# Three weight-sharing projection chunks, scores by key block and a later flag read in a fused attention kernel

## The chip, the cores and the metric

The kernel runs on one core of a Trainium2 chip. The metric is the device time of one execution in microseconds (us). A timed execution is 1.8 us longer than the span that its profile shows from the first to the last instruction.

The engines: PE (TensorE) multiplies, PEld is its weight load, ACT is ScalarE, DVE is VectorE, POOL is GpSimd, SP is SyncE, which here issues all 611 DMAs. Each engine has a program of its own.

## The reference

```python
B, Sq, D = 8, 112, 640
H, Sk, Dh = 32, 512, 192
q = (x @ wq).reshape(B, Sq, H, Dh).transpose(0, 2, 1, 3)
scores = einsum("bhqd,bhkd->bhqk", q, k_cache) * Dh ** -0.5
o = einsum("bhqk,bhkd->bhqd", softmax(scores), v_cache)
out = o.transpose(0, 2, 1, 3).reshape(B, Sq, H * Dh) @ wo
```

All is bf16. The key and value caches are 50 MB each, so about 118 MB have to be read.

## The kernel before

The work is cut into 64 units (8 groups of 4 heads, times 8 batches). For each unit DVE transposes four key blocks, PE makes scores, ACT takes the exponential, PE multiplies by the values, and output and projection matmuls of other groups fill in. POOL copies three quarters of each unit's values into a padded tile and reorders projection weights. The program starts with the projection of group 0, in six chunks `c` of two halves `h`. It ends with a check flag: each engine reads it and branches to the end, or to a slower second program if a row sum was out of range.

```python
def get_flag(eng):                        # every engine's last act
    W(eng, vT, 3)                         # W = wait for a semaphore
    eng.reg_load(regs[eng.engine], flag[0:1, 0:1])
...
def do_Q0_first():                        # PE: chunks 0 and 1, first half
    for dc in range(DC):                  # five pieces of weights
        W(pe, mW0[dc], 16)                # landed?
        for c in range(2):
            for a in range(4):            # one "group" of four matmuls
                ... pe.matmul(ps[32*a:32*a+32, 6 + c, 0:HQ], ...)
def do_Q0(c, h):                          # the other chunks
    W(pe, aQ, n - 1)                      # ACT has emptied the bank of chunk n-2
    ... into bank 6 + n % 2               # chunks 4, 5 use weights that POOL reorders
...
def do_S(u):                              # PE: scores of unit u
    W(pe, vKT, 4 * (u + 1))               # for unit 0: all four key blocks
    W(pe, aEX, 4 * u)                     # all exponentials of unit u-1
...
def exp(u, a):                            # ACT
    W(act, pS, 4 * u + a + 1)
    if a == 3 and u >= 2:
        W(act, gM, u + 1)                 # POOL has copied unit u's values
...
def middle(u):                            # POOL: that copy
    W(gp, mV[u % NV], 64 * (u // NV + 1)) # the values have landed
...
# POOL's loop: reorder projection weights placed at u, then a check, then middle(u + 2)
EARLY_LOADS = ("k1", "q", "v0", "k2", "v1", "k3", "o", "v2")   # SP's order of issue after k0
```

Of the kernel before, what the change touches and what calls it, by code (L numbers as in the profile page):

```python
# [666 lines left out]
def build_main(nc, x, k_cache, v_cache, wq, wo, out, flag, regs, hints):  # L667
# [8 lines left out]
    HQ = R // 2  # L676
# [19 lines left out]
    o_list = [(g, m, h) for g in range(NG) for m in range(MT) for h in range(2)]  # L696
# [61 lines left out]
    with ExitStack() as es:  # L758
# [7 lines left out]
        xT = sb("xT", [128, DC, R], BF16)  # L766
        wqs = sb("wqs", [128, 2, DC, 4 * DH], BF16)
# [6 lines left out]
        qT = [sb(f"qT{j}", [128, 6, R], BF16) for j in range(2)]  # L774
# [3 lines left out]
        wq0 = oT[:].rearrange("p c r -> p (c r)")[:, 0:DC * 4 * DH].rearrange("p (d w) -> p d w", d=DC)  # L778
# [11 lines left out]
        ps = es.enter_context(nc.psum_tensor("ps", [128, 8, 512], F32))  # L790
# [11 lines left out]
        aX, aEX, aQ, aT, aNM = (sem(n) for n in ("aX", "aEX", "aQ", "aT", "aNM"))  # L802
# [14 lines left out]
        def W(eng, s, v):  # L817
            if v > 0:
                eng.wait_ge(s, v)

        def bank_free(eng, pair, h):
# [3 lines left out]
            else:  # L825
                W(eng, vO, o_index[g, c, h] + 1)

        def last_unit(m):
            return -(-128 * (m + 1) // SQ) - 1

        def get_flag(eng):
            W(eng, vT, 3)
            eng.reg_load(regs[eng.engine], flag[0:1, 0:1])

        def on_tensor(pe):
            def do_X(m):
                if m in (0, 2, 4):
                    W(pe, mX[x_piece[m]], 16)
                if m == 6:
                    W(pe, aQ, 5)  # L840
                for dc in range(DC):
                    mm = pe.transpose(psb[:, 5 if m == 3 and dc >= 2 else m, dc * 128:(dc + 1) * 128], xs[:, m, dc * 128:(dc + 1) * 128], ident[:])  # L842
                mm.then_inc(pXT, 1)
# [8 lines left out]
            def do_Q0_first():  # L852
                W(pe, vX, 3)
                W(pe, aX, 2)
                for dc in range(DC):
                    W(pe, mW0[dc], 16)
                    for c in range(2):
                        for a in range(4):
                            w0 = DH * a + 64 * (c // 2) + c % 2
                            mm = pe.matmul(ps[32 * a:32 * a + 32, 6 + c, 0:HQ], wqs[:, 0, dc, w0:w0 + 63:2],  # L860
                                           xT[:, dc, 0:HQ], start=(dc == 0), stop=(dc == DC - 1))
                        if dc == DC - 1:
                            mm.then_inc(pQ, 1)

            def do_Q0(c, h):
                n = q_index[0, c, h]
                if c == 0:
                    W(pe, vX, 4)
                    W(pe, aX, 4)
                W(pe, aQ, n - 1)  # L870
                for dc in range(DC):
                    if h == 1 or c >= RAW:
                        if h == 0 and c == RAW:
                            W(pe, gW0, dc + 1)
                        mm = pe.matmul(ps[:, 6 + n % 2, 0:HQ], wq0[:, dc, 128 * c:128 * (c + 1)], xT[:, dc, HQ * h:HQ * (h + 1)],  # L875
                                       start=(dc == 0), stop=(dc == DC - 1))
                        continue
                    for a in range(4):
                        w0 = DH * a + 64 * (c // 2) + c % 2
                        mm = pe.matmul(ps[32 * a:32 * a + 32, 6 + n % 2, 0:HQ], wqs[:, 0, dc, w0:w0 + 63:2],  # L880
                                       xT[:, dc, HQ * h:HQ * (h + 1)], start=(dc == 0), stop=(dc == DC - 1))
                mm.then_inc(pQ, 1)

# [37 lines left out]
            def do_S(u):  # L921
                g, b = divmod(u, B)
                if u < 3 or kt_ahead[u - 2][0] + min(3, kt_ahead[u - 2][1] - kt_ahead[u - 2][0]) < 4 * (u + 1):
                    W(pe, vKT, 4 * (u + 1))
                if b == 0 or u == 4:
                    W(pe, aQ, q_index[g, 5, b // 4 if g == 0 else 1] + 1)
                W(pe, aEX, 4 * u)
                if u == 0:
                    W(pe, vX, 3)
                    W(pe, aX, 2)  # L930
                for t in range(4):
                    for c in range(6):
                        for a in range(4):
                            p = slice(32 * a, 32 * a + 32)
                            mm = pe.matmul(ps[:, a, SQ * t:SQ * (t + 1)], kt[u % NT][p, t, c // 2, :, c % 2],  # L935
                                           qT[g % 2][p, c, SQ * b:SQ * (b + 1)], start=(c == 0), stop=(c == 5))
                            if t == 3 and c == 5:
                                mm.then_inc(pS, 1)
# [36 lines left out]
            for j in range(BRIDGE):  # L975
                (held if j else pe.matmul)(ps[:, 7, 0:128], wt[:], wt[:], True, True)
            do_Q0_first()
            for c in range(2, 6):
                do_Q0(c, 0)
            for m in range(4, MT):  # L980
                do_X(m)
# [21 lines left out]
        def on_scalar(act):  # L1003
            W(act, vI, 1)
            act.activation(dmy[:, 1:2], dmy[:, 0:1], ACTF.Exp)

            def evac_x(m, n=DC):
                W(act, pXT, m + 1)
                act.activation(xT[:, 0:n, 128 * m:128 * (m + 1)],
                               psb[:, m, 0:128 * n].rearrange("p (c s) -> p c s", c=n), ACTF.Copy).then_inc(aX, 1)  # L1010

            def evac(g, c, h):
                n = q_index[g, c, h]
                W(act, pQ, n + 1)
                if g >= 2 and c == 0 and h == 0:
                    W(act, pS, 4 * B * (g - 1))
                act.activation(qT[g % 2][:, c, HQ * h:HQ * (h + 1)], ps[:, 6 + (n % 2 if g == 0 else h), 0:HQ],  # L1017
                               ACTF.Copy).then_inc(aQ, 1)

            def evac_pair(i, j):  # L1020
                if slot[i, j] and slot[i, j][0][0] == "Q" and slot[i, j][1] != FRONT:
                    for h in range(2):
                        evac(*slot[i, j][0][1:], h)

            def exp(u, a):
                W(act, pS, 4 * u + a + 1)
                if a == 3 and u >= 2:
                    W(act, gM, u + 1)
                if a == 0:
                    W(act, pPV, u - 1)  # L1030
                    if u < 2:
                        W(act, gV, 1)
                act.activation(pT[u % 2][:, a, :, 0:SQ], ps[:, a, 0:4 * SQ].rearrange("p (t q) -> p t q", t=4), ACTF.Exp,  # L1033
                               scale=scale).then_inc(aEX, 1)

            def norm(u):
                W(act, vRC, u + 1)
                W(act, pT_, u - 1)
                for e in range(2):
                    ins = act.activation(os_[u % 2][:, DH * (2 + e):DH * (3 + e)], pv_of(u)[0:SQ, 1, e, 0:DH], ACTF.Copy,  # L1040
                                         scale=rinv[:, u % 4, 2 + e:3 + e])
                ins.then_inc(aNM, 1)

            def tevac(u):
                g, b = divmod(u, B)
                W(act, pT_, u + 1)
                if g > 0:
                    W(act, pO, 2 * (MT * (g - 1) + (SQ * b + SQ - 1) // 128 + 1))
                src = psb[:, bank_of_T(u), 2:2 + 4 * RW].rearrange("p (k w) -> p k w", k=2)[:, :, 0:3 * SQ]
                act.activation(oT[:, :, SQ * b:SQ * (b + 1)].rearrange("p (k c) q -> p k c q", k=2),  # L1050
                               src.rearrange("p k (c q) -> p k c q", c=3), ACTF.Copy).then_inc(aT, 1)

            evac_x(1)
            evac_x(3, 2)
            for c in range(6):
                evac(0, c, 0)
            for m in (4, 5):
                evac_x(m)
            for c in range(6):
                if c < 4:  # L1060
                    exp(0, c)
                evac(0, c, 1)
            for i in range(1, NU + 2):
                if i == HINT_AT["act"]:
                    hints[mybir.EngineType.Activation] = act.mark_branch_hint_location()
                if i < NU:
                    exp(i, 0)
                if i >= 2:
                    tevac(i - 2)
                if i < NU:  # L1070
                    exp(i, 1)
                evac_pair(i, 0)
                if i < NU:
                    exp(i, 2)
                    exp(i, 3)
                if 1 <= i <= NU:
                    norm(i - 1)
                evac_pair(i, 1)
            get_flag(act)
# [276 lines left out]
```

## Time and profile before

| | before |
|---|---|
| timed runs at first, median (range) | 396.77 us (396.52 to 397.45) |
| span of the profile | 396.5 us |
| PE busy | 387.3 us |
| first projection matmul to first score matmul | 7.68 us |
| end of the last output addition to the end of the span | 3.05 us |
| issue of the last output DMA | 1.39 us (that of the one before: 0.33) |

From the page of the profile of the kernel before: the span, the busy times, and the chain that ended last as shares of the span.

```profile
span 396.5 us, 19831 instructions
...
PE 387.3 (98%) x8865; PEld 242.6 (61%) x8262; DVE 283.2 (71%) x506; ACT 250.6 (63%) x550; POOL 153.3 (39%) x352
...
PE 97%; issue 1%; DMA 1%; DVE 1%; ACT 0%
```

PE is busy almost always, and the chain of what released what hardly leaves it.

The chain of waits of the kernel before, 3 to 17 us, in order of time: start, duration, what. L860 is `do_Q0_first`, L880 and L875 the other chunks, L842 the transposes of x, L935 the scores, L1017 the eviction of a chunk by ACT.

```profile
6.54 2.22 PE ps L860 x36
8.75 0.02 issue
8.78 0.55 ACT qT L1017
9.33 0.04 issue
9.37 2.08 PE ps L880 x40
11.45 2.00 PE ps L875 x10
13.45 0.84 PE ps L842 x15
14.29 1.04 PE ps L935 x75
15.33 0.76 issue
```

Two holes: PE stands from 8.75 to 9.37 us while ACT empties the first bank, and for 0.76 us inside the first scores, where the chain names no releaser ("issue").

The end, from the timeline of the kernel before: SP's last DMA issue (start, duration).

```profile
393.50 1.39 SPq L1299 DMA_DIRECT2D out_dram<-xs  x1
```

And the DMA view of the kernel before from 393.45 us on: packets of the instruction queue q8, and the one issue in this stretch with its time to landing.

```profile
q8 instruction: 1, 0.02, 1.8%
...
out_dram<-xs SPq DMA_DIRECT2D x1, 64.0 KB, 2.9
```

One packet of 16384 bytes falls on the same time as the last issue (it starts at 393.50 and takes 1.05 us), and the output needs 2.9 us to land. I take q8 for PE's instruction queue: it has 69 packets in the run, all of 16384 bytes, and six gaps of PE inside its scores follow such a packet: PE goes on 2.25 to 3.2 us after its start (median 2.5). All six lie at the same place when PE's 17180 records are counted off in 256s (at 193 to 195), and 17180 divided by 256 makes 67. I call these gaps packet gaps (the recorded texts say fetch gaps, or instruction fetch). That PE stands there for want of the packet is read from the coincidence in time and place.

### The profile page before, as it was taken

What the parts mean: (1) busy time and instruction counts of PE and PEld (TensorE: products, weight loads), DVE (VectorE), ACT (ScalarE), POOL (GpSimd) and SP (SyncE); (2) the same over time, 40 slices, a digit from 0 to 9 for tenths busy, and PEclk for the clock granted to TensorE, in tenths of its full rate; (3) what the DMA queues carried; (4) which work ended last, traced back from release to release, by engine and by line L of the source; (5) the groups of instructions that cost most, each with busy time, mean ns of one, the idle gap of its engine ahead of it and who ended that gap; (6) DMA issues with size and microseconds to landing.
All of it is one profiled execution on the core that took longest, in us unless ns stands there. A gap on an engine that the chain in (4) does not pass through costs nothing.

```text
span 396.5 us, 19831 instructions
## 1 busy us (share of the span) xinstructions
PE 387.3 (98%) x8865; PEld 242.6 (61%) x8262; DVE 283.2 (71%) x506; ACT 250.6 (63%) x550; POOL 153.3 (39%) x352
## 2 busy tenths in 40 slices
PE   7999999999999999999999999999999999999995
PEld 2555665656656656666666656666566665667672
DVE  1664778677796777776787676876678677789733
ACT  3667665757647765657755666566764766667562
POOL 5433454233442354334342255233454223334420
PEclk9999999999999999999999999999999999999999
DMA  8999999999999999899999999999999889989712
GB/s 263 376 370 374 355 302 366 331 311 351 323 367 292 311 309 358 282 312 304 306 293 345 307 275 337 365 275 317 282 292 345 257 271 317 339 274 297 254 35 72
DMA packets 88588, 120.04 MB, mean 303 GB/s; under 512 B 9776, under 2 KB 88496, under 8 KB 88496
## 3 DMA queue, kind: packets, MB, share of 16 engines
q1 hardware_dynamic: 88496, 118.72, 91.0%
q8 instruction: 69, 1.13, 1.2%
q14 instruction: 23, 0.19, 0.2%
HBM read 117.54 MB, written 1.15 MB: 299 GB/s over the span
## 4 chain that ended last, share of the span: by engine, by line
PE 97%; issue 1%; DMA 1%; DVE 1%; ACT 0%
PE ps L953 22%; PE ps L916 22%; PE ps L846 22%; PE ps L935 21%; PE ps L964 6%; PE ps L875 2%; DMA xs<-in_x_dram 1%; PE ps L842 1%; PE ps L860 1%; PE ps L880 1%; DVE xs L1115 0%; DVE xT L1120 0%; ACT qT L1017 0%
## 5 line engine op out<-in xcount | busy, mean ns | idle before, releaser
L1092 DVE STREAM_TRANSPOSE kt<-kr 128x384 int32<-128x384 int32 x256 | 195.4, 871 | 9.7 <-DMA kr<-in_k_cache_dram 9.7
L1033 ACT ACTIVATE pT<-ps 128x448 bf16<-128x448 f32 x256 | 130.4, 559 | 85.2 <-PE ps L935 85.1
L935 PEld LDWEIGHTS ps<-qT,kt 32*128 32x128 bf16 x6144 | 77.3, 93 | 33.3 <-issue 23.1
L916 PE MATMUL ps<-wos,oT 128*128 128x320 bf16 (+2 forms) x342 | 93.0, 298 | 0.7 <-DVE xs L1115 0.7
L1212 POOL TENSOR_SCALAR bad<-rinv 112x4 f32<-112x4 f32 x64 | 14.7, 230 | 201.7 <-DVE rinv L1098 201.7
L953 PE MATMUL ps<-vm,pT 128*128 128x193 bf16 x768 | 91.5, 247 | 0.2
L935 PE MATMUL ps<-qT,kt 32*128 32x112 bf16 x6144 | 88.6, 208 | 2.8 <-issue 2.8
L846 PE MATMUL ps<-wos,oT 128*128 128x320 bf16 (+1 forms) x340 | 91.3, 296 | 0.0
L953 PEld LDWEIGHTS ps<-vm,pT 128*128 128x128 bf16 x768 | 67.8, 97 | 21.2 <-ACT oT L1050 11.1
L1195 POOL COPY vm<-vs 128x1152 int32<-128x1152 int32 x64 | 73.5, 1149 | 13.3 <-issue 6.2
L846 PE MATMUL ps<-xT,wqs 128*128 128x448 bf16 (+2 forms) x226 | 74.1, 341 | 0.0
L916 PE MATMUL ps<-xT,wqs 128*128 128x448 bf16 (+1 forms) x210 | 73.5, 350 | 0.0
L1040 ACT ACTIVATE os<-ps,rinv 112x192 bf16<-112x192 f32 x128 | 48.0, 437 | 28.5 <-DVE rinv L1098 28.5
L953 PE MATMUL ps<-vs,pT 128*128 128x193 bf16 x256 | 62.6, 245 | 0.0
L916 PEld LDWEIGHTS ps<-wos,oT 128*128 128x128 bf16 x342 | 33.2, 97 | 43.8 <-issue 36.7
L1017 ACT ACTIVATE qT<-ps 128x448 bf16<-128x448 f32 x96 | 47.9, 552 | 18.9 <-PE ps L916 12.3
L1115 DVE TENSOR_TENSOR acc<-ps,acc 128x320 f32<-128x320 f32 x84 | 37.3, 486 | 26.3 <-PE ps L916 26.0
L1050 ACT ACTIVATE oT<-ps 128x672 bf16<-128x672 bf16 x64 | 46.4, 725 | 2.1 <-PE ps L964 2.1
L1098 DVE RECIPROCAL rinv<-ps 112x4 f32<-112x4 f32 x64 | 11.1, 174 | 50.1 <-PE ps L953 50.1
L916 PEld LDWEIGHTS ps<-xT,wqs 128*128 128x128 bf16 x210 | 20.3, 97 | 34.2 <-issue 29.4
L1101 DVE TENSOR_TENSOR os<-ps,rinv 112x384 bf16<-112x384 f32 x64 | 35.7, 558 | 7.3 <-DVE rinv L1098 0.5
L1188 POOL COPY wqs<-wqr 128x384 bf16<-128x384 bf16 x70 | 33.4, 511 | 5.4 <-DMA wqr<-in_wq_dram 5.4
(44 smaller groups left out, 155.1 us busy)
## 6 DMA issues: line engine op xcount, KB each, us to landing
kr<-in_k_cache_dram SPq DMA_DIRECT2D x256, 192.0 KB, 4.2
vs<-in_v_cache_dram SPq DMA_DIRECT2D x256, 192.0 KB, 4.1
wos<-in_wo_dram SPq DMA_DIRECT2D x48, 160.0 KB, 4.3
wqr<-in_wq_dram SPq DMA_DIRECT2D x35, 192.0 KB, 5.3
wqs<-in_wq_dram SPq DMA_DIRECT2D x5, 192.0 KB, 4.6
out_dram<-xs SPq DMA_DIRECT2D x6, 160.0 KB, 2.5
xs<-in_x_dram SPq DMA_DIRECT2D x2, 320.0 KB, 3.5
xs<-in_x_dram SPq DMA_DIRECT2D x1, 480.0 KB, 5.7
```

What stands on the lines that cost most here:

```text
L846: return pe.add_instruction(mybir.InstMatmult(name=nc.get_next_instruction_name(), engine=mybir.EngineType.PE, ins=[pe.lower_ap_or_imm(rhs ...
L916: mm = (pe.matmul if h == hs[0] and f == 0 else held)(ps[:, 6 + h, cs], w, rhs[h][:, cs], q == 0, q == n - 1 and f == cuts - 1)
L935: mm = pe.matmul(ps[:, a, SQ * t:SQ * (t + 1)], kt[u % NT][p, t, c // 2, :, c % 2], qT[g % 2][p, c, SQ * b:SQ * (b + 1)], start=(c == 0), ...
L953: mm = pe.matmul(pv[:, k, e, 0:DH + 1], pT[u % 2][:, a, t, :], src[:, a, v0:v0 + DH + 1], start=(t == 0), stop=(t == 3), skip_group_check= ...
L1017: act.activation(qT[g % 2][:, c, HQ * h:HQ * (h + 1)], ps[:, 6 + (n % 2 if g == 0 else h), 0:HQ], ACTF.Copy).then_inc(aQ, 1)
L1033: act.activation(pT[u % 2][:, a, :, 0:SQ], ps[:, a, 0:4 * SQ].rearrange("p (t q) -> p t q", t=4), ACTF.Exp, scale=scale).then_inc(aEX, 1)
L1040: ins = act.activation(os_[u % 2][:, DH * (2 + e):DH * (3 + e)], pv_of(u)[0:SQ, 1, e, 0:DH], ACTF.Copy, scale=rinv[:, u % 4, 2 + e:3 + e])
L1050: act.activation(oT[:, :, SQ * b:SQ * (b + 1)].rearrange("p (k c) q -> p k c q", k=2), src.rearrange("p k (c q) -> p k c q", c=3), ACTF.Co ...
L1092: dve.transpose(dst, src).then_inc(vKT, 1)
L1101: dve.tensor_tensor(os_[u % 2][:, 0:2 * DH].rearrange("p (e d) -> p e d", e=2), pv[0:SQ, 0, :, 0:DH], rinv[:, u % 4, 0:2][:, :, None].broa ...
L1115: ins = dve.tensor_tensor(ob[:, m, cs] if g == NG - 1 else acc[:, m, cs], src, acc[:, m, cs], op=ALU.add)
L1195: gp.tensor_copy(vm[u % NM][:].rearrange("p a (t w) -> p a t w", w=RW)[:, :, :, 0:DH].bitcast(I32), vs[u % NV][:, :, 32:32 + 3 * DH].rearr ...
```

## The change

The intent: let three chunks use each piece of weights as it lands, in three banks, so that PE needn't wait for an eviction; let the first scores wait for one key block at a time; and keep every engine from reading the flag until the last output addition.

```diff
+        def bank_of_Q0(n):
+            return (6, 7, 0, 5, 4, 7)[n] if n < 6 else 6 + n % 2
         def get_flag(eng):
+            W(eng, vO, len(o_list))
             W(eng, vT, 3)
@@ do_X
-                if m == 6:
+                if m in (4, 5, 6):
                     W(pe, aQ, 5)
@@ do_Q0_first
-                    for c in range(2):
+                    for c in range(3):
...  (6 + c, 6 + n % 2 become bank_of_Q0, in ACT's eviction too)
@@ do_Q0
-                W(pe, aQ, n - 1)
+                W(pe, aQ, (0, 0, 0, 0, 0, 2)[n] if n < 6 else n - 1)
@@ do_S
-                    W(pe, vKT, 4 * (u + 1))
+                    W(pe, vKT, 4 * (u + 1) if u else 1)
...
                 for t in range(4):
+                    if u == 0:
+                        W(pe, vKT, t + 1)
@@ PE's order
-            for c in range(2, 6):
+            for c in range(3, 6):
                 do_Q0(c, 0)
```

More of the change, by code (lines that the diff above doesn't have):

```diff
@@ L856, in do_Q0_first @@
                     W(pe, mW0[dc], 16)
-                    for c in range(2):
+                    for c in range(3):
                         for a in range(4):
                             w0 = DH * a + 64 * (c // 2) + c % 2
-                            mm = pe.matmul(ps[32 * a:32 * a + 32, 6 + c, 0:HQ], wqs[:, 0, dc, w0:w0 + 63:2],
+                            mm = pe.matmul(ps[32 * a:32 * a + 32, bank_of_Q0(c), 0:HQ], wqs[:, 0, dc, w0:w0 + 63:2],
                                            xT[:, dc, 0:HQ], start=(dc == 0), stop=(dc == DC - 1))
@@ L874, in do_Q0 @@
                             W(pe, gW0, dc + 1)
-                        mm = pe.matmul(ps[:, 6 + n % 2, 0:HQ], wq0[:, dc, 128 * c:128 * (c + 1)], xT[:, dc, HQ * h:HQ * (h + 1)],
+                        mm = pe.matmul(ps[:, bank_of_Q0(n), 0:HQ], wq0[:, dc, 128 * c:128 * (c + 1)], xT[:, dc, HQ * h:HQ * (h + 1)],
                                        start=(dc == 0), stop=(dc == DC - 1))
@@ L879, in do_Q0 @@
                         w0 = DH * a + 64 * (c // 2) + c % 2
-                        mm = pe.matmul(ps[32 * a:32 * a + 32, 6 + n % 2, 0:HQ], wqs[:, 0, dc, w0:w0 + 63:2],
+                        mm = pe.matmul(ps[32 * a:32 * a + 32, bank_of_Q0(n), 0:HQ], wqs[:, 0, dc, w0:w0 + 63:2],
                                        xT[:, dc, HQ * h:HQ * (h + 1)], start=(dc == 0), stop=(dc == DC - 1))
@@ L1016, in evac @@
                     W(act, pS, 4 * B * (g - 1))
-                act.activation(qT[g % 2][:, c, HQ * h:HQ * (h + 1)], ps[:, 6 + (n % 2 if g == 0 else h), 0:HQ],
+                act.activation(qT[g % 2][:, c, HQ * h:HQ * (h + 1)], ps[:, bank_of_Q0(n) if g == 0 else 6 + h, 0:HQ],
                                ACTF.Copy).then_inc(aQ, 1)
```

## The prediction

> **What bounds the kernel now.** The tensor engine (PE). The page gives PE busy 387.3 of 396.5 us, clock granted 1.0, and the chain of waits is 97% PE. The instruction records show only twelve PE gaps over 0.04 us. Six of them (2.8 us) are inside the score matmuls and follow the 16 KB packets of the instruction queue by about 2.45 us; the rest lie in the first 10 us and the last 8. After 17 us PE never stands still for a load, so a shift of PE's start should reach the end.
>
> **Start (timeline and chain, 4 to 17 us).** The weights of the first projection land at 5.80, 6.33, 7.31, 7.81, 8.31 us, and two chunks (2 groups of four matmuls, 0.208 us a group by the third and fourth chunks: 2.08 us for 10) consume each: 6.54 to 8.75. PE's weight load waits 0.31 to 0.38 us for the last three. Then the chain leaves PE: chunk 2 waits for the first ACT eviction (8.78 to 9.33) and starts at 9.37. Projection ends 13.45, transposes 14.29, then scores.
> With three chunks in three banks the first pass is 15 groups, 3.12 us: each weight costs 0.62 us, more than the 0.50 between arrivals, so waits vanish: 6.54 to 9.66. Chunks 3 and 4 have own banks and no eviction wait; chunk 5's bank 7 is free by about 10.3. PE runs through to about 12.70, transposes to 13.54. New limits do not bind by my sum: POOL's reordered weights end 10.50 (chunk 4 starts 10.70); x's last piece lands 11.75 (needed 12.70); chunk 4's eviction ends about 12.3; chunk 5's at 13.3. Scores start about 13.55 instead of 14.29: gain 0.75 us. The key transposes end at 11.2, 11.95, 12.7, 13.44, so waiting per key block gains about nothing[...]. The 0.76 us gap in the first scores[...] should stay. Next consumers have slack: keys of unit 2 are ready 1.8 us before use.
>
> **End (trace's DMA and SyncE records, 390 to 396.5 us).** ACT, POOL and PE read the flag at 391.55 and branch at 392.1 while output is still coming. PE's branch is followed by a 16 KB instruction packet at 393.50 (1.05 us). The last output's DMA issue starts at 393.50 and takes 1.387 us instead of 0.33; it lands at 396.37 and ends the span. Throughout the run long DMA issues (1 to 2 us against 0.43) coincide with these packets. One piece of the output before has a straggler (395.57 against 394.61). [...] The change moves the branches behind the last addition (393.47): flag read to about 394.05, PE's packet about 395.4, after the last issue (now done at 393.83) and about at its landing (393.83+1.45=395.3). Gain about 1.05 us of span. [...]
>
> **Sum.** 396.77-0.7-0.95: about 395.1 us; 8 in 10: 394.4 to 396.2. Faster by over 2%: 0.005; within: 0.99; slower: 0.005.
>
> **What would show it.** No PE gap near 9.4 and scores starting near 13.5; weight-load waits on the first weights gone; the last output issue near 0.33 us, no instruction packet between 392 and 395; the last addition about 0.7 us earlier and the span 1.7 shorter.
>
> **What would make it wrong.** Instruction packets falling elsewhere and stalling scores or issues by another 1 us; the flag-waiters' packets hitting the last landing; a new wait of the transposes for evictions; loads limiting units 1 to 3, giving the 0.7 back.

The sum came to 396.77 - 0.7 - 0.95 = 395.1 us. In it 0.75 us of the start count as 0.7, and 1.05 us of the end as 0.95.

## The result, and the profile after

| | before | after |
|---|---|---|
| median of 6 runs (range) | 396.63 us (395.40 to 397.45) | 394.86 us (394.36 to 395.59) |
| span of the profile | 396.5 us | 392.6 us |
| first projection to first scores | 7.68 us | 6.74 us |
| last addition to end | 3.05 us | 1.71 us |
| gaps of PE inside score matmuls, sum | 2.83 us | 1.92 us |

The ratio is 0.9964, 95% interval 0.9943 to 0.9986. A ratio is the mean time of one kernel's runs over the mean of the other's from the same rounds, so it is not quite the ratio of the medians in the table. The two profiles differ by 3.9 us, more than twice the timed difference: the profile of before fell on an execution slower than all six timed ones (398.36 us), that of after on the fastest of its six (394.36). So the two spans must not simply be subtracted.

From the page of the profile after, the same lines.

```profile
span 392.6 us, 19835 instructions
...
PE 385.5 (98%) x8865; PEld 242.2 (62%) x8262; DVE 283.2 (72%) x506; ACT 250.7 (64%) x550; POOL 153.0 (39%) x352
...
PE 91%; SPq 3%; issue 2%; DMA 2%; DVE 1%; POOL 0%; ACT 0%; ACTq 0%
```

PE's share of the chain fell from 97% to 91%, and SP's queue and a DMA came in. This is the line to stop at: the chain's beginning is no longer PE's.

PE's timeline of the kernel after, 6.6 to 13.6 us (L864 is `do_Q0_first`, L884 and L879 the other chunks, L846 the transposes, L941 the scores).

```profile
6.74 3.02 PE L864 MATMUL ps<-xT,wqs 128*32 128x448 bf16 x60
9.59 1.12 PE L884 MATMUL ps<-xT,wqs 128*32 128x448 bf16 x20
10.64 2.06 PE L879 MATMUL ps<-xT,oT 128*128 128x448 bf16 x10
12.54 1.00 PE L846 MATMUL ps<-ident,xs 128*128 128x128 bf16 x15
13.47 0.33 PE L941 MATMUL ps<-qT,kt 32*128 32x112 bf16 x12
```

No hole is left in this stretch. Sixty matmuls take 3.02 us, and the next chunks follow at once.

The timeline of the kernel after, SP's last issue.

```profile
390.87 0.33 SPq L1305 DMA_DIRECT2D out_dram<-xs  x1
```

The DMA view of the kernel after from 390.85 us on.

```profile
out_dram<-xs SPq DMA_DIRECT2D x1, 64.0 KB, 1.5
```

The issue takes 0.33 us instead of 1.39, and the output lands 1.5 us after the issue began instead of 2.9. PE's instruction packet comes only at 392.76, when the output has landed (392.40).

So both ends changed as they were meant to. But the chain of waits of the kernel after, 17 to 34 us, reads like this (many issues of SP left out; L1301 is SP's issue of loads, L1201 POOL's copy, L1039 the exponential):

```profile
23.92 0.43 SPq L1301
24.35 0.04 issue
24.39 1.10 DMA vs<-in_v_cache_dram
25.49 4.87 issue
30.36 1.15 POOL vm L1201
31.52 0.02 issue
31.54 0.02 ACTq L819
31.56 0.04 issue
31.60 0.55 ACT pT L1039
32.16 0.14 issue
32.29 1.21 PE ps L941 x82
```

Read it upwards. The scores of unit 3 (32.29) waited for the last exponential of unit 2, that one for POOL's copy of unit 2's values, the copy for those values to land (30.25), and the load had been issued from 22.97 us on because SP had been issuing one DMA after another since 0.7 us. SP's order of issue is not the whole of it: the last of these four DMAs was issued at 24.39 us and landed 5.9 us later (the first x, issued at 0.74, took 3.8), and from 20 to 30 us the 16 DMA engines were fully taken (busy share 1.07, 371 GB/s), so the transfers probably stood in line too. No work of PE is in this chain before 32.29 us, so it doesn't depend on when PE started. The question for the experiments was how much of the start's gain goes through it.

### The profile page after: what moved, and what is told of

It reads as the page before. It is cut to its first block, busy times and chain, and to the rows that moved or that the text cites. A ratio compares the mean times of both kernels' runs of the same rounds, so it can differ in the third digit from the quotient of the medians.

```text
span 392.6 us, 19835 instructions
## 1 busy us (share of the span) xinstructions
PE 385.5 (98%) x8865; PEld 242.2 (62%) x8262; DVE 283.2 (72%) x506; ACT 250.7 (64%) x550; POOL 153.0 (39%) x352
## 4 chain that ended last, share of the span: by engine, by line
PE 91%; SPq 3%; issue 2%; DMA 2%; DVE 1%; POOL 0%; ACT 0%; ACTq 0%
PE ps L959 22%; PE ps L920 21%; PE ps L850 21%; PE ps L941 20%; PE ps L970 6%; SPq L1301 3%; DMA kr<-in_k_cache_dram 2%; DVE kt L1098 1%; DVE xs L1121 0%; POOL vm L1201 0%; DMA vs<-in_v_cache_dram 0%; ACT pT L1039 0%; ACTq L819 0%
## 5 line engine op out<-in xcount | busy, mean ns | idle before, releaser
L1039 ACT ACTIVATE pT<-ps 128x448 bf16<-128x448 f32 x256 | 130.6, 560 | 83.1 <-PE ps L941 82.6
L941 PEld LDWEIGHTS ps<-qT,kt 32*128 32x128 bf16 x6144 | 77.1, 93 | 31.6 <-issue 21.6
L941 PE MATMUL ps<-qT,kt 32*128 32x112 bf16 x6144 | 87.5, 208 | 1.9 <-issue 1.5
L1201 POOL COPY vm<-vs 128x1152 int32<-128x1152 int32 x64 | 73.5, 1148 | 17.4 <-issue 9.4
```

Source lines behind the costliest of these rows:

```text
L941: mm = pe.matmul(ps[:, a, SQ * t:SQ * (t + 1)], kt[u % NT][p, t, c // 2, :, c % 2], qT[g % 2][p, c, SQ * b:SQ * (b + 1)], start=(c == 0), ...
L1039: act.activation(pT[u % 2][:, a, :, 0:SQ], ps[:, a, 0:4 * SQ].rearrange("p (t q) -> p t q", t=4), ACTF.Exp, scale=scale).then_inc(aEX, 1)
L1201: gp.tensor_copy(vm[u % NM][:].rearrange("p a (t w) -> p a t w", w=RW)[:, :, :, 0:DH].bitcast(I32), vs[u % NV][:, :, 32:32 + 3 * DH].rearr ...
```

## The experiments

Theory A: the end gives 1.0 to 1.3 us, the start 0.7 to 0.9, the rest of the 3.9 us between the profiles is chance. Rivals: all comes from the start (C); the first packet gap is a fixed cost of the old start (B). Later: the start's gain is given back to loads (E), or to a packet gap (F).

Every profile gives exact times inside one execution of the kernel, while a timed ratio is good to 0.2 to 0.4% only. In the tables "start" is first projection matmul to first score matmul, "tail" is last addition's end to the end of the span.

### A control: before_again

No edit.

> The kernel before, unchanged, as a control. Ratio to itself 1.000 within 0.2%. Theory A (the change saves 0.7 to 0.9 us in the first projection and 1.0 to 1.3 us after the last addition, and the rest of the 3.9 us between the two profiles is chance in the instruction fetch): first projection matmul to first score matmul 7.6 to 7.7 us, last addition's end to the end of the span about 3.0 us, last output issue 1.4 us; the sum of PE gaps inside score matmuls may differ from 2.8 us by half a microsecond or more, and the 0.76 us gap in the first unit's scores may be there or not. Rival B (that first gap is a fixed cost of the kernel before that the change removes): the gap is again 0.7 to 0.8 us at the same matmul.

Ratio 0.9989 (0.9962 to 1.0017), so a kernel against itself. Start 7.98 us, tail 2.90 us, last issue 1.32 us. The gaps inside scores sum to 1.24 us here, not 2.83: a second profile of the same kernel differs by 1.6 us in this alone. The gap in the first scores is there, 0.44 us instead of 0.76, after the same number of PE instructions (record 449 of PE's in both, counted from 0 with its waits). Its place is fixed, its length is not, and tail_only below, with the same start, has no such gap: rival B falls as far as it calls the gap a fixed cost.

### The end: tail_only, front_only, pe_leaves, pe_stays_alone

tail_only is the kernel before with one line:

```diff
         def get_flag(eng):
+            W(eng, vO, len(o_list))
```

> The kernel before with only the wait for all output additions before the flag read. Theory A: tail from 3.05 to about 1.7 us, last output issue 0.33 us, start as before (7.6 to 7.7 us from first projection to first scores); time 1.0 to 1.3 us under before, ratio about 0.997. Rival C: no change, ratio 1.000 within 0.1%.

front_only is the change without that line.

> The changed kernel without its wait for all output additions before the flag read. Theory A: first projection matmul to first scores stays at 6.7 us, last addition's end to the end of span goes back to about 3.0 us with a last output issue near 1.4 us; time about 0.8 to 1.0 us under before, ratio 0.997 to 0.998. Rival C (the wait at the end does nothing, all of the gain is the start): ratio 0.9955 to 0.9965 as for the whole change, tail 1.7 us.

pe_leaves is the change, where PE alone does not wait:

```diff
-            W(eng, vO, len(o_list))
+            if eng.engine != mybir.EngineType.PE:
+                W(eng, vO, len(o_list))
```

> The changed kernel, but the tensor engine alone does not wait for the output additions before its flag read; the other four do. Theory A (the tensor engine's branch calls a 16 KB instruction packet, and that packet holds up the issue of the last output): last output issue 1.3 to 1.4 us again, tail from last addition to end of span 2.9 us. Rival D (the early flag reads and branches of ScalarE and GpSimd are the cost): tail 1.7 us as in the change.

pe_stays_alone is the kernel before, where PE alone waits (the same line with `==`).

> The kernel before, with only the tensor engine waiting for all output additions. Theory A: last output issue 0.33 us, tail 1.7 to 1.9 us, start as before. Rival D: tail 2.9 to 3.05 us. Start: first projection to first scores 7.6 to 8.0 us as in the three profiles with the old start, and a fetch gap in the first unit's scores of 0 to 0.8 us.

| | start | PE waits at end | others wait | last issue, us | tail, us | ratio to before |
|---|---|---|---|---|---|---|
| before_again | old | no | no | 1.32 | 2.90 | 0.9989 |
| front_only | new | no | no | 1.44 | 2.89 | 0.9992 (0.9959 to 1.0025) |
| pe_leaves | new | no | yes | 1.29 | 3.60 | 1.0020 (0.9993 to 1.0047) |
| pe_stays_alone | old | yes | no | 0.57 | 2.12 | 0.9960 (0.9937 to 0.9983) |
| tail_only | old | yes | yes | 0.33 | 1.71 | 0.9960 (0.9929 to 0.9991) |
| after, after_again | new | yes | yes | 0.33 | 1.71 | 0.9964, 0.9977 |

The timeline of pe_leaves, SP's last issue.

```profile
392.89 1.29 SPq L1306 DMA_DIRECT2D out_dram<-xs  x1
```

The timeline of pe_stays_alone, SP's last issue.

```profile
394.66 0.57 SPq L1301 DMA_DIRECT2D out_dram<-xs  x1
```

PE's leaving is what holds up the last issue: with it 1.29 us, without it 0.57 or 0.33. The trace's packet list suggests how: PE's branch is followed by a 16384-byte packet (393.50 in before, 392.81 in pe_leaves), and the issue that overlaps it takes a microsecond longer. Over the whole run the two go together: of before's 61 issues over 0.8 us, 59 overlap such a packet; of after's 51, all. But 34 other issues of before overlap one and stay short. So that PE's leaving costs the time is shown by experiment; that it does so through the packet is read from the coincidence in time, and no run tests it apart. The packet starts 0.7 us after PE's branch ends in both (392.78 and 392.08). The rest of pe_stays_alone's tail (0.4 us over tail_only) goes with the smaller packets that follow the branches of ACT and POOL (8192 bytes each, at 394.29 and 394.41 us), and its profile fell on its slowest execution (398.52 us), so that rest is not settled. In pe_leaves, whose tail is longer than before's, the others' small packets (394.59 to 394.79) now come just before the last output lands, and its last piece took until 396.30; whether the one causes the other is not shown.

Over before, before_again and front_only the tail averages 2.95 us, in every profile where all engines wait it is 1.71 or 1.72: 1.24 us saved. And front_only's ratio is the surprise: the new start alone shows no gain (0.9992), while either kernel that only keeps PE at the end has the whole change's gain. Rival C falls. The part of theory A about the start is in doubt.

front_only's profile also had bad luck. PE's timeline of front_only, 4 to 9.6 us:

```profile
4.51 2.29 PE L845 MATMUL ps<-ident,xs 128*128 128x128 bf16 x20 [0.76 <-DMA xs<-in_x_dram]
...
7.58 2.26 PE L863 MATMUL ps<-xT,wqs 128*32 128x448 bf16 x24
```

The first twenty transposes, 1.5 us from first to last in after with a wait for x inside, take 2.29 us, and 24 matmuls take 2.26 us, where after does 60 in 3.02: 0.094 us each against 0.050, about half speed. The trace's record of a full granted clock opens at 9.54 us in this run, and at 3.76 to 6.22 us in the other eleven profiles that have one, a scatter of 2.5 us; I call this the clock's release. Before shows that the speed changes there: its record opens at 5.26 us, and its transposes start 0.107 us apart until then and 0.056 us apart after it. In after, whose record opens at 4.05 us, before the first transpose, they start 0.056 us apart from the first on, but for the wait for x. Why the release came so late in front_only is not shown. Against after this cost 1.0 us between the first transpose and the projection (3.07 against 2.07) and 0.9 from there to the scores (7.67 against 6.74).

### The start: two_chunks_own_banks, keys_at_once, after_again

two_chunks_own_banks is the change, but the third chunk follows in its own bank instead of sharing the arrivals:

```diff
-                    for c in range(3):        # do_Q0_first
+                    for c in range(2):
-            for c in range(3, 6):
+            for c in range(2, 6):
                 do_Q0(c, 0)
```

> The changed kernel, but only two chunks share each weight arrival; the third chunk comes after them, in bank 0, without a wait for an eviction. If the gain at the start comes from the bank (no wait for ACT) alone: first projection to first scores as in the change, 6.7 us. If sharing the arrivals counts too: 7.0 to 7.15 us (the eviction's 0.6 us saved of 7.67, the weight waits back at 0.1 us each and a slower first pass). Time between the change and 0.4 us above it, which the timing will hardly resolve; the profile decides.

Start 7.45 us, more than the 7.0 to 7.15 expected, but so was the time of the weights: the third, fourth and fifth piece landed at 7.14, 8.21 and 8.72 us, against 6.96, 7.46 and 7.98 in after. PE's weight loads waited 0.84 us for the fourth piece and 0.39 for the fifth. With those arrivals three chunks (0.19 us a group) would have ended the first pass, chunk 2 included, at about 9.4 us by my sum (8.25 + 6 groups), where this kernel ended chunk 2 at 10.1. So sharing counts as well as the bank: about 0.6 us for the eviction that nobody waits for, and 0 to 0.7 for the arrivals, more the later they come. The sizes are sums, not runs, but tail_v2_first below, an old start whose weights never kept PE waiting, agrees: 7.38 us, 0.64 more than after. Ratio 0.9946 (0.9914 to 0.9978).

keys_at_once is the change without the waits by key block:

```diff
-                    W(pe, vKT, 4 * (u + 1) if u else 1)
+                    W(pe, vKT, 4 * (u + 1))
-                    if u == 0:
-                        W(pe, vKT, t + 1)
```

> The changed kernel with the first scores waiting for all four key blocks at once. Where the key transposes end before the first scores start (13.1 against 13.5 us in the profile of the change) nothing changes: first projection to first scores 6.7 to 6.8 us with the clock full. Where the keys land 0.5 us later, up to 0.4 us is lost. Ratio to the change within noise.

Start 6.90 us, with a gap of 0.10 us before the first scores, as the key transposes ended at 13.21 and PE was ready then. In after_again, whose transposes ended only at 13.51, the scores began at 13.05 and nothing was lost. So the waits by block are worth 0.1 to 0.5 us at the start when keys are late, nothing otherwise (the 0.5 is a sum: 13.51 less 13.05). Ratio 0.9984 (0.9953 to 1.0015), not told apart from the change.

after_again has no edit.

> The changed kernel once more, on the chip of the three others. Ratio to before 0.995 to 0.998. Profile: first projection to first scores 6.7 to 7.0 us if the clock is released before the projection starts (it was not in front_only, which lost about 1.8 us there), tail 1.7 us, first unit's scores 1.36 us long without a fetch gap.

Start 6.74 us, tail 1.71, first scores 1.36 us long, ratio 0.9977 (0.9951 to 1.0002). All as expected, but one gap was not: 2.05 us before the scores of unit 3. The view of waits of after_again, PE, 20 to 40 us (who waited for whom: total, times, longest):

```profile
PE ps L941 <- ACT pT L1039: 2.0, 1, 2.0
```

The timeline of after_again at that time, POOL and ACT (in brackets the idle time before, and what ended it).

```profile
31.41 1.15 POOL L1201 COPY vm<-vs 128x1152 int32<-128x1152 int32 x1 [4.72 <-issue]
...
32.65 0.54 ACT L1039 ACTIVATE pT<-ps 128x448 bf16<-128x448 f32 x1 [2.20 <-POOL vm L1201]
```

PE waits for ACT, ACT for POOL's copy, and POOL for the values, which landed at 31.30 us (the view says "issue" for a copy that really waited for its DMA, since POOL's wait stands in an instruction of its own).

### Where the start's gain goes

The trace gives the first score matmul of every unit. Old start above, new start below, all with the old order of loads:

| us | unit 0 | unit 1 | values of unit 2 landed | their copy ended | unit 3 | unit 9 |
|---|---|---|---|---|---|---|
| before | 14.22 | 22.25 | 31.05 | 32.30 | 33.55 | 69.70 |
| before_again | 14.07 | 21.79 | 30.33 | 31.59 | 32.37 | 68.40 |
| tail_only | 13.75 | 20.92 | 30.29 | 31.55 | 32.33 | 68.09 |
| pe_stays_alone | 14.36 | 22.21 | 30.68 | 31.94 | 33.78 | 70.73 |
| front_only | 15.26 | 22.33 | 30.71 | 31.97 | 32.75 | 69.14 |
| after | 13.47 | 20.55 | 30.25 | 31.51 | 32.29 | 68.60 |
| after_again | 13.05 | 20.12 | 31.30 | 32.56 | 33.34 | 68.66 |
| keys_at_once | 13.27 | 20.34 | 30.99 | 32.25 | 33.03 | 68.35 |
| pe_leaves | 12.78 | 19.85 | 30.62 | 31.88 | 32.66 | 68.42 |
| two_chunks_own_banks | 13.98 | 21.06 | 31.11 | 32.36 | 33.14 | 68.46 |

At unit 1 the new start is ahead by 1.7 us on the median (20.34 against 22.00, front_only with its late clock release left out). At unit 3 it is ahead by nothing: in eight of the ten profiles unit 3 starts 0.78 us after the end of POOL's copy, whatever happened before. Only before and pe_stays_alone, the two with the longest packet gaps until then, come later than that. front_only, which began its scores 2.2 us later than after_again, reached unit 3 0.6 us earlier, since its values landed earlier. From unit 9 on all kernels have the same pace: unit 9 to 16 takes 40.54 us in most of them, and what differs are mostly single packet gaps.

To try it, the values of unit 2 were issued earlier.

after_v2_first, one edit to the change:

```diff
-    EARLY_LOADS = ("k1", "q", "v0", "k2", "v1", "k3", "o", "v2")
+    EARLY_LOADS = ("k1", "q", "v0", "k2", "v1", "k3", "v2", "o")
```

> The changed kernel with one change of load order: the values of unit 2 are issued before the six pieces of the first output weights, not after. Theory E (the time saved at the start is given back at the scores of unit 3, which wait through the last exponential of unit 2 for the copy of unit 2's values, and that load lands at 30 to 31 us whatever PE does): the values of unit 2 land near 27 to 28 us instead of 30.3 to 31.3, scores of unit 3 start at 31 to 31.7 us instead of 32.3 to 33.3 and no longer 0.78 us after the copy's end, scores of unit 8 start at 60 to 61.2 us instead of 61.4 to 62.1, and the time is 0.7 to 1.5 us under the change's, ratio to before 0.993 to 0.995. Rival F (the gap in unit 3's scores is instruction fetch, as the profile's label 'issue' suggests): unit 3 starts no earlier than before, and the time is that of the change.

The values landed at 28.45 us, their copy ended at 29.71, and unit 3 started at 31.36, free of it: the timeline of after_v2_first shows its scores in one piece, with no idle time before them.

```profile
31.36 1.36 PE L941 MATMUL ps<-qT,kt 32*128 32x112 bf16 x96
```

Unit 8 started at 60.11, 1.3 us before the earliest of the other new starts (61.41). Theory E holds and F falls for this gap. But then unit 8 took 8.64 us instead of 6.56, and unit 9 started at 68.75 again. The view of waits of after_v2_first, PE, 60 to 70 us:

```profile
PE ps L920 <- POOL wqs L1194: 1.9, 1, 1.9
```

The timeline of after_v2_first, POOL, 55 to 68 us:

```profile
64.66 1.14 POOL L1201 COPY vm<-vs 128x1152 int32<-128x1152 int32 x1 [4.01 <-issue]
65.74 0.95 POOL L1194 COPY wqs<-wqr 128x384 bf16<-128x384 bf16 x2
```

The next projection needed the last reordered weights, and that reorder stood in POOL's program behind the copy of unit 8's values, which landed at 64.55. The gain was given back once more in this profile, to another load, again by way of POOL's order of work. How much is given back there varies: the values of unit 8 landed at 61.59 to 64.93 us in the fourteen profiles, and only one was later than this one. Ratio to before 0.9929 (0.9899 to 0.9958), median 394.38 us.

tail_v2_first is tail_only with the same new order of loads.

> The kernel before with the wait at the end and the same new load order, so it lacks only the new start. Theory E: unit 3 is no longer held by the values of unit 2; with nothing else in the way the old start now shows: unit 8 starts 0.6 to 1.2 us later than in after_v2_first, time as much longer. If the new start is worth nothing in itself, both are equal at unit 8.

Unit 8 started at 62.22, 2.1 us after after_v2_first, more than the 0.6 to 1.2 expected, as its profile had 1.6 us of packet gaps until then (0.50 and 1.13) where after_v2_first had 0.15. At unit 9 both were equal (68.79 and 68.75). Ratio 0.9983 (0.9949 to 1.0017): the new order alone gives the old start nothing that could be seen.

The timed runs of these two, taken on one chip, say more than their two profiles. They don't overlap: 393.46 to 394.85 us for after_v2_first, 395.19 to 397.51 for tail_v2_first, means 1.9 us apart (give or take 1.1, an estimate from the scatter of six runs each). With the old order nothing of the kind is seen in pairs on one chip that differ in the start (nearly alone): front_only less before_again is +0.3 us in the mean, two_chunks_own_banks less tail_only -0.4, after_again less pe_stays_alone -0.1, each good only to 1 us or more. So the new start does reach the end, at least in part, once the values of unit 2 come first, as theory E says. The two profiles, equal at unit 9, don't show where; that of after_v2_first fell on its slowest of six.

after_o_last moves the first output weights behind the values of unit 3 too.

```diff
+    EARLY_LOADS = ("k1", "q", "v0", "k2", "v1", "k3", "v2")
@@ later loads
                     load_v(u - 1)
+                if u == 4:
+                    for c in range(3):
+                        load_wo(0, c)
```

> As after_v2_first, but the first output weights go behind the keys of unit 4 and the values of unit 3 as well. Values of unit 3 land near 33 us instead of 34.5 to 35.4. If the next limit after unit 2's values is unit 3's values (scores of unit 4 start at the earliest about 2 us after they land, 36.5 to 37.4 us), this gains up to 0.5 us more on after_v2_first; if the first output additions now wait for their weights at 38 to 41 us, it loses as much. My guess: equal within 0.3 us.

The values of unit 3 landed at 31.95, earlier than the 33 us expected, but the profile can't answer its question: unit 3 had a packet gap of 1.96 us, after which PE's granted clock fell to 0.50 from 35.2 to 38.6 us, and unit 4 started at 41.15. Ratio 0.9930 (0.9900 to 0.9960), as after_v2_first. Inconclusive.

after_v2_reorder is after_v2_first with POOL's last reorder of each group one unit earlier, so ahead of the copy:

```diff
-    at.setdefault(8 * (g - 1) - 5 + dc if g >= 2 else -1, [])
+    at.setdefault(8 * (g - 1) - 5 + min(dc, 3) if g >= 2 else -1, [])
```

> after_v2_first with one more edit: GpSimd reorders the last piece of each group's projection weights one unit earlier, so ahead of its copy of the values that come next. In after_v2_first PE stood still 1.90 us at 66.75 us for that reorder, which stood behind the copy that waited for the values of unit 8 to land at 64.55. Theory E (the time saved at the start is given back to loads, by way of whichever in-order engine waits for them, unit 3 first and unit 8 next): no gap there, scores of unit 9 start near 66.7 us instead of 68.3 to 68.8, unit 16 near 107.2 instead of 108.6 to 109.7, and from there the same pace as all the others; time 1.5 to 2 us under after_v2_first and 2 to 2.5 us under the change, ratio to before 0.987 to 0.992. If the values of unit 9 or 10 hold it up next, unit 16 starts at 109 again and nothing is gained.

The gap at unit 8 was gone (6.56 us again), unit 9 started at 66.73, 2.0 us before after_v2_first, as expected. Unit 15 then took 6.93 us instead of 6.30, so unit 16 started at 107.90. PE's weight loads waited 0.44 us at 105.9 for an output addition of DVE. DVE had stood 1.59 us for the keys of unit 16 (landed 98.49) and 0.64 us for those of unit 17 (landed 103.95), with that addition behind them in its program: a load again. The span, 391.4 us, is the shortest of all profiles. In time it did less than the 0.987 to 0.992 expected: median 394.91 us (393.18 to 395.55), ratio 0.9929 (0.9893 to 0.9966), as after_v2_first. Both new versions have a lower ratio to before than the change (0.9964 and 0.9977), but the intervals overlap, and none ran beside the change on one chip. That they beat it in time is not shown.

## Why the prediction was right, and where it was not

The time was right: 395.1 us predicted, 394.86 measured, within the range. But the sum got there with two wrong terms, one too large and one too small, so in part by luck.

- **What bounds the kernel.** PE with 97% of the chain, right for this profile. The conclusion drawn from it, "After 17 us PE never stands still for a load, so a shift of PE's start should reach the end", is the step that failed. PE did not stand still for a load because it was late itself. In before the copy of unit 2's values ended at 32.30 us and unit 3 started at 33.55; it could have started at 33.08 (0.78 later), so 0.47 us of slack, less than the shift; in before_again and tail_only, with the old start too, there was none.
- **"Next consumers have slack: keys of unit 2 are ready 1.8 us before use."** True of the keys. The values were not looked at, and they bound, by way of POOL and ACT. "Loads limiting units 1 to 3, giving the 0.7 back" stood among the things that could make it wrong, and that is what happened.
- **Start, the local part.** 0.75 us expected between projection and scores; 0.94 measured (7.68 to 6.74), right in mechanism: no eviction wait, no weight waits, POOL and x in time. "The 0.76 us gap in the first scores should stay" was wrong: the first unit's scores took 1.36 to 1.43 us in all nine profiles of the new start, and 1.45 to 2.32 us in the five of the old. The instruction packet before them starts 1.7 to 2.7 us after PE passes its record 193 with the new start, and 2.8 to 3.6 with the old. Why it starts sooner is not settled. None of it reaches the end.
- **End.** 1.05 us of span expected, 1.24 measured (2.95 to 1.71): 1.05 from the issue (1.39 to 0.33) and 0.28 from landing sooner after the issue's end (1.48 to 1.20), in the profiles of before and after. That PE's early leaving is the cost is shown by pe_leaves and pe_stays_alone; that its instruction packet is the means rests on the coincidence in time. Nothing was lost after the end of the span: time and span differ by 1.8 us in both kernels.
- **Sum.** Predicted 0.7 + 0.95. Measured about 1.2 to 1.4 from the end and, with the old order of loads, nothing resolvable from the start: the six runs in which PE waits at the end, with the old order of loads, have ratios that average 0.9965, and the three without it 1.0000, a difference of 1.4 us. Of the six, the two with the old start average 0.9960 and the four with a new one 0.9968. With the values of unit 2 first, the start showed 1.9 us between after_v2_first and tail_v2_first.
- **Key blocks.** "Gains about nothing" in the typical case; up to 0.5 us at the start if keys land late (after_again), then given back too.

What stays open: why executions of one kernel differ, by 1.2 us (after, the first six) to 4.6 us (before on one chip, 395.24 to 399.79). Gaps inside scores (0.3 to 3.9 us in a profile, after packets or for loads) and the moment of the clock's release go some way, but they were not separated in the timed runs.

## What to carry to other kernels

Before a gain at the start of a kernel is put into the sum, every stream that the later stages consume has to be checked against it, also those that reach the busy engine through two others; an engine at 98% busy may be exactly as late as its loads. Here the view by windows of before gives the 16 DMA engines a share of 1.03 to 1.07 in every 5 us from 5 to 40, which a look at it beforehand would have told. A unit start that keeps a constant distance from another engine's event over many profiles (0.78 us here) points to such a limit. And at the end of a program, an engine that is done early is not free: in all four profiles where PE left early, a 16384-byte packet fell on the last output's issue, and that issue took 1.29 to 1.44 us.

## What the traces show of packets, issues and the clock

- Most instruction packets of PE go with no gap (six gaps inside scores for 69 packets in before), but not all: PE stood 0.3 to 3.9 us of a run inside its scores, part of it after packets. In before all six gaps lie at the same place of every 256 records (records 449, 961, 1219, 3267, 16323 and 16579 of PE's, counted from 0 with its waits, equal to within 2 when multiples of 256 are taken off). From each such place (record 193 and every 256 on) to the start of its packet, paired in order, the median is 1.9 us.
- An instruction packet and a slow DMA issue of another engine go together: the median of SP's issues is 0.43 us, and in before 61 of 611 take 0.8 to 2.4 us; 59 of those overlap a 16384-byte packet (51 of 51 in after), but 34 short ones overlap one too.
- PE's early leaving cost time at another engine's last output: 1.24 us of tail, by the means of three profiles without PE's wait or any other and those with all waits.
- The clock's release was recorded at 3.76 to 6.22 us from the start of the span, and once at 9.54. PE stood still in between, from the end of the matmuls before x at 3.8 us to between 3.9 and 4.7 us.
